# Re-placing the weight loads at the layer boundary of a two-layer decode kernel, and cutting its second query projection into three column groups

## The chip, the cores and the metric

The kernel runs on one core of one Trainium2 chip. The metric is the device time of one execution in microseconds (us). Most executions of one kernel agree within about 0.3%. Ratios below are computed as the mean time of one kernel's fast runs over that of the other's of the same rounds, so they are not quite the ratio of the medians that are quoted beside them.

In the profile lines PE is the matrix engine, PEld its weight loads, DVE the vector engine, ACT the scalar engine, POOL the GpSimd engine, and SP the engine on whose queue the loads are issued; L102 is line 102 of that kernel. 16 DMA engines move the bytes. "issue" is time in which an engine waited for nothing that the profile shows. A load has landed when all its bytes are there.

## The reference, cut to what matters

One token goes twice through an attention block and a gated feed-forward block, with the same weights and the same caches both times. Only the last 4096 of 32768 cache positions count.

```python
# D = 640, 32 heads of 192, window W = 4096, F = 1536, bf16
def _A_ref(x, k_cache, v_cache, wq, wo):
    q = (x @ wq).reshape(B, Sq, Hq, Dh) ...
    k = k_cache[:, :, Sk - W:, :]; v = v_cache[:, :, Sk - W:, :]
    scores = einsum("bhqd,bhkd->bhqk", q, k) * (Dh ** -0.5)
    o = einsum("bhqk,bhkd->bhqd", _softmax(scores), v)
    return o ... @ wo
def _B_ref(x, w1, w3, w2):
    return (_silu(x @ w1) * (x @ w3)) @ w2
x = x + _A_ref(_layernorm(x), ...); x = x + _B_ref(_layernorm(x), ...)
x = x + _A_ref(_layernorm(x), ...); x = x + _B_ref(_layernorm(x), ...)
```

K and V of the window are 100.7 MB together. They do not fit on the core, so most of them are loaded once for each layer.

## The kernel before

Heads go in four blocks of eight (b), each in four pairs (z). One large tile `pg` holds everything that is loaded: a work area for the probabilities, an area `AUX` for wo, a strip that keeps 20 of the 64 positions per partition of one V pair for the second layer, and seven slots of one K or V pair each (3 MB). Every load has a planned place. One function issues all of them, in one fixed order, on the SP queue. A load waits there until the readers of what was in its place are done, and all later loads wait behind it:

```python
    def need(key):
        while key not in place:
            k, at, n, src = queue.pop(0)
            ...
            nc.sync.dma_start(out=pg[:, at:at + n], in_=src)
```

The first layer handles its blocks in the order 0, 1, 2, 3 and the second in the order 3, 2, 1, 0. The K pairs of block 3 and most of its V are kept, so they fill all seven slots while the kernel passes from the first layer to the second. In that time the loads must live in the 12,288 columns below the kept strip: first wo of block 3, then w1, w3, w2 and the second layer's wq.

```python
    plan_cut(("wo", 0, 3), D, CUT_WO, wo_v[3], AUX)               # AUX = 4096
    plan_ffn(0, ((0, QCH, 2 * QCH), (7680, 0, 10752), QCH))       # w1, w3, w2; QCH = 3072
    for half, ring in ((1, (0, 1, 2, 3, 0)), (0, (1, 2, 3, 0, 1))):
        for c in range(NCH):                                      # wq in 10 chunks of 768 KB
            o = 6144 * c + 3072 * half
            plan(("wq", 1, half, c), QCH * ring[c], QCH, wq_v[:, o:o + 3072])
    ...
    plan_k(1, 2, 0, 1)      # the first K pair that the second layer loads: into slot 1
    ...
    wst = cst.tile([P, NZ, 2, 6, 36], BF16, name="wst")           # q, spread out as matmul weights
    ptm, e, et = pg[:, 0:2048], pg[:, 2048:3072], pg[:, 3072:4096]   # the work area
```

The second layer starts like this. The first half of wq (blocks 2 and 3) gives the weights `wst` for block 3, whose K is there already; `qproj_tail`, the "q tail", is the copy and the transposing matmuls that stand between. Each `k_stage` scores one kept K pair with 24 matmuls and so frees that pair's slot. The chunks of the other half are multiplied before and inside the first stage:

```python
            q_mms(q_ps[1], 1, (0,))
            st, rstd = statistics()
            q_mms(q_ps[1], 1, range(1, NCH))
            qproj_tail(q_ps[1], 1, rstd)
            q_mms(q_ps[0], 0, (0, 1))
            build_w(order[0])
            for z in range(NZ):
                between = [(6 + 4 * i, lambda c=c: q_mms(q_ps[0], 0, (c,))) for i, c in enumerate((2, 3))]
                k_stage(order[0], z, s_ps, z == 0, z == NZ - 1, between if z == 0 else ())
                if z == 0:
                    q_mms(q_ps[0], 0, (4,))
                    work_area()
```

## Time and profile before

| | |
|---|---|
| median time | 537.48 us (6 runs, 536.04 to 538.25) |
| span of the profiled run | 534.3 us; that run took 536.04 us, the shortest of all |
| loaded | 222 MB |
| rate in the steady parts | 420 to 440 GB/s |

Lines of the page of the kernel before: the span; the busy share of the DMA engines and their rate in 40 equal slices; the main queue; the chain of waits by engine.

```profile
span 534.3 us, 6605 instructions
...
DMA  8999999999999999999999989999999999999995
GB/s 353 442 423 426 440 422 432 436 421 434 430 423 425 438 429 437 424 426 430 418 355 397 400 339 422 424 434 425 432 430 423 434 429 432 432 428 429 417 409 222
...
q1 hardware_dynamic: 15554, 221.59, 98.1%
...
DMA 61%; DVE 15%; PE 13%; issue 7%; ACT 3%; SPq 1%; another core or an unknown queue 0%; ACTq 0%; DVEq 0%
```

The DMA engines are busy nearly always, and the rate is level but for slices 21 to 24 (355, 397, 400, 339), which is 267 to 321 us: the layer boundary. A closer look at it, in the kernel before. Each line is a stretch of 3 us; the last two numbers are the share of the DMA engines and GB/s, the number before them is the granted clock of PE.

```profile
273.00:276.00 3.00, 1.30 (x25) 1.07 (x22) 0.90 (x2) 0.48 (x1) 0.00 (x0) 0.50 0.86 301
276.00:279.00 3.00, 2.17 (x50) 2.04 (x51) 0.56 (x3) 0.00 (x0) 0.00 (x0) 0.50 0.87 278
291.00:294.00 3.00, 1.62 (x37) 1.46 (x35) 0.57 (x3) 0.00 (x0) 0.00 (x0) 0.50 1.00 353
294.00:297.00 3.00, 2.19 (x18) 1.05 (x19) 0.69 (x4) 0.41 (x2) 0.00 (x0) 0.50 0.97 381
312.00:315.00 3.00, 3.00 (x24) 1.01 (x20) 1.34 (x1) 0.00 (x0) 0.00 (x0) 1.00 0.58 160
315.00:318.00 3.00, 3.00 (x16) 0.83 (x14) 0.00 (x0) 0.00 (x0) 0.00 (x0) 1.00 0.84 360
```

These are three holes. When the loads were issued says why. This is the timeline of the SP queue of the kernel before (start, duration of the group from its first issue to its last, what, how many):

```profile
251.47 2.34 SPq L102 DMA_DIRECT2D pg<-in_A_v_cache_dram  x3
253.86 1.53 SPq L102 DMA_DIRECT2D pg<-in_A_wo_dram  x3
273.19 12.69 SPq L102 DMA_DIRECT2D pg<-in_B_w_dram  x9
287.35 18.09 SPq L102 DMA_DIRECT2D pg<-in_A_wq_dram  x10
306.98 0.33 SPq L102 DMA_DIRECT2D pg<-in_A_wo_dram  x1
312.95 0.56 SPq L102 DMA_DIRECT2D pg<-in_A_k_cache_dram  x1
```

And these are the longest waits of that queue between 270 and 330 us, in the kernel before (total us, times, longest):

```profile
SPq L102 <- PE s_ps L318: 20.1, 4, 5.6
SPq L102 <- PE o_ps L363: 17.7, 1, 17.7
```

Nothing is issued between 255 and 273 us, because w1's place is the work area, and the last matmul that reads the probabilities (`o_ps`) is still to come. In the second hole the second q load waits until 291.10 us, for the first two pieces of w2 to be multiplied. The K load at 312.95 waits for the first K stage (`s_ps`).

### The profile page before, as it was taken

To read this page: it belongs to the slowest core of one execution; us is meant where nothing else is said; L and a number is where in the kernel's file an instruction comes from. 1 tells how busy PE (TensorE), PEld (TensorE's weight loads), DVE (VectorE), ACT (ScalarE), POOL (GpSimd) and SP (SyncE) were. 2 spreads that over 40 slices of the span, in tenths; PEclk is the share of its full clock that TensorE was granted. 3 is DMA by queue.
4 is the path that set the end of the run, shared out by engine and by line. 5 is a ranking of instruction groups with operands and counts; after the bars stand their busy time and mean duration, and the time that the engine had idled before them with its cause. 6 is when DMAs were issued, how large, how long until landed. Compare 5 with 4: busy or idle time off the path is not lost.

```text
span 534.3 us, 6605 instructions
## 1 busy us (share of the span) xinstructions
PE 292.2 (55%) x2934; PEld 124.5 (23%) x2934; DVE 247.0 (46%) x287; ACT 37.9 (7%) x90; POOL 8.7 (2%) x38
## 2 busy tenths in 40 slices
PE   2427655550764416946366598584773425945475
PEld 1201111110321112213135232221321112312153
DVE  3169974426475074553011116788475175553011
ACT  0100020001100020002000001101100020002000
POOL 6000000000000000000000000000000000000000
PEclk9998877765678758867556599987777757977657
DMA  8999999999999999999999989999999999999995
GB/s 353 442 423 426 440 422 432 436 421 434 430 423 425 438 429 437 424 426 430 418 355 397 400 339 422 424 434 425 432 430 423 434 429 432 432 428 429 417 409 222
DMA packets 15726, 222.00 MB, mean 416 GB/s; under 512 B 1873, under 2 KB 1874, under 8 KB 7378
## 3 DMA queue, kind: packets, MB, share of 16 engines
q1 hardware_dynamic: 15554, 221.59, 98.1%
q8 instruction: 23, 0.38, 0.3%
q14 instruction: 5, 0.04, 0.0%
q10 hardware_dynamic: 144, 0.00, 0.0%
HBM read 221.58 MB, written 0.00 MB: 415 GB/s over the span
## 4 chain that ended last, share of the span: by engine, by line
DMA 61%; DVE 15%; PE 13%; issue 7%; ACT 3%; SPq 1%; another core or an unknown queue 0%; ACTq 0%; DVEq 0%
DMA pg<-in_A_k_cache_dram 43%; DVE pg L310 10%; PE s_ps L318 7%; DMA pg<-in_A_v_cache_dram 6%; DMA pg<-in_B_w_dram 5%; DMA pg<-in_A_wo_dram 5%; PE y_ps L395 3%; DMA pg<-in_A_wq_dram 2%; ACT pg L340 2%; DVE pg L343 1%; PE o_ps L363 1%; DVE wst L302 1%; ACT pg L351 1%; SPq L102 1%; PE z_ps L470 1%
## 5 line engine op out<-in xcount | busy, mean ns | idle before, releaser
L310 DVE STREAM_TRANSPOSE pg<-pg 128x1536 uint32<-128x1536 uint32 x112 | 189.1, 1746 | 108.5 <-DMA pg<-in_A_k_cache_dram 108.4
L318 PE MATMUL s_ps<-pg,wst 128*32 128x512 bf16 x768 | 174.6, 615 | 109.6 <-DVE pg L310 105.8
L318 PEld LDWEIGHTS <-wst 128*32 128x32 bf16 x768 | 47.2, 116 | 219.8 <-issue 202.9
L363 PE MATMUL o_ps<-pg 128*16 128x384 bf16 (+1 forms) x1024 | 75.1, 377 | 21.3 <-DMA pg<-in_A_v_cache_dram 18.2
L363 PEld LDWEIGHTS <-pg 128*16 128x16 bf16 (+1 forms) x1024 | 31.4, 97 | 51.9 <-issue 39.7
L340 ACT ACTIVATE pg<-s_ps,nbt 32x512 bf16<-32x512 f32 x16 | 13.2, 822 | 369.8 <-DVE nbt L337 369.6
L380 PE MATMUL ot_ps<-o_sb,csel 128*128 128x192 bf16 x16 | 3.5, 317 | 64.6 <-ACT o_sb L377 64.6
L395 PE MATMUL y_ps<-otd,pg 128*128 128x1 bf16 x540 | 23.3, 178 | 12.5 <-DVE otd L387 6.8
L282 PE MATMUL q_ps<-pg,xs 128*32 128x384 bf16 x160 | 16.5, 495 | 21.9 <-DMA pg<-in_A_wq_dram 21.9
L395 PEld LDWEIGHTS <-pg 128*128 128x128 bf16 x540 | 23.1, 131 | 14.5 <-issue 8.0
L384 DVE SCALAR_TENSOR_TENSOR om<-ot_ps,rl,dsel 128x192 f32<-128x192 f32 x8 | 3.1, 386 | 36.9 <-PE ot_ps L380 36.9
L372 DVE RECIPROCAL rl<-rl_ps 128x1 f32<-128x1 f32 x8 | 1.3, 168 | 38.0 <-PE rl_ps L370 38.0
L380 PEld LDWEIGHTS <-csel 128*128 128x128 bf16 x16 | 1.6, 99 | 68.1 <-issue 68.1
L343 DVE STREAM_TRANSPOSE pg<-pg 128x1024 bf16<-128x1024 bf16 x8 | 10.0, 1245 | 15.2 <-ACT pg L340 15.2
L351 ACT COPY pg<-pg 32x256 bf16<-32x256 bf16 x32 | 13.6, 424 | 8.0 <-DVE pg L343 7.5
L282 PEld LDWEIGHTS <-xs 128*32 128x32 bf16 x160 | 6.5, 123 | 28.4 <-issue 17.2
L298 DVE TENSOR_SCALAR qt_sb<-qt_ps,rstd 128x96 bf16<-128x96 f32 x4 | 1.3, 318 | 19.5 <-PE qt_ps L295 19.5
L328 DVE TENSOR_REDUCE t<-s_ps 128x1 f32<-128x512 f32 x8 | 5.2, 646 | 11.0 <-PE s_ps L318 11.0
L353 DVE COPY pg<-pg 32x256 bf16<-32x256 bf16 x32 | 9.2, 287 | 0.6
L434 PE MATMUL u_ps<-xn,pg 128*128 128x1 bf16 x120 | 7.7, 198 | 3.3 <-DMA pg<-in_B_w_dram 3.3
L434 PEld LDWEIGHTS <-pg 128*128 128x128 bf16 x120 | 7.4, 160 | 4.2 <-DMA pg<-in_B_w_dram 4.2
L222 POOL MEMSET pg<- 128x128 f32 x1 | 0.2, 204 | 481.9 <-PE o_ps L363 481.9
(73 smaller groups left out, 84.0 us busy)
## 6 DMA issues: line engine op xcount, KB each, us to landing
pg<-in_A_k_cache_dram SPq DMA_DIRECT2D x28, 3072.0 KB, 40.6
pg<-in_A_v_cache_dram SPq DMA_DIRECT2D x25, 3072.0 KB, 37.0
pg<-in_A_wo_dram SPq DMA_DIRECT2D x5, 1920.0 KB, 34.5
pg<-in_A_wq_dram SPq DMA_DIRECT2D x10, 768.0 KB, 6.8
pg<-in_A_wq_dram SPq DMA_DIRECT2D x2, 3072.0 KB, 13.3
pg<-in_A_wo_dram SPq DMA_DIRECT2D x9, 640.0 KB, 21.4
pg<-in_B_w_dram SPq DMA_DIRECT2D x7, 768.0 KB, 11.4
pg<-in_A_v_cache_dram SPq DMA_DIRECT2D x2, 2112.0 KB, 17.2
```

The costliest lines, as they stand in the source:

```text
L102: nc.sync.dma_start(out=pg[:, at:at + n], in_=src)
L282: nc.tensor.matmul(q_ps[32 * j:32 * j + 32, 0:384], lhsT=xs4[:, c, c2, :], rhs=w[:, o:o + 384], start=(c == 0 and cl == 0), stop=(c == NCH ...
L302: nc.vector.tensor_tensor(out=_ap(wst[:], 0, P, 4 + 216 * h, [[433, NZ], [36, 6], [8, 4]]), in0=_ap(qt_sb[:], 0, P, 96 * h + 4 * b, [[1, N ...
L310: nc.vector.transpose(v, v)
L318: nc.tensor.matmul(s_ps[64 * h:64 * h + 32, :], lhsT=wst[:, z, h, it, 4 - 4 * th:36 - 4 * th], rhs=_ap(x, 0, P, 192 * th + 64 * be + par + ...
L340: nc.scalar.activation(out=_ap(e, 64 * h, 32, h, [[32, 32], [2, 16]]), in_=s_ps[r, :].rearrange("p (t j) -> p t j", j=16), func=ACTF.Exp, ...
L343: nc.vector.transpose(et, e)
L351: nc.scalar.copy(out=dst, in_=src)
L353: nc.vector.tensor_copy(out=dst, in_=src)
L363: nc.tensor.matmul(o_ps[32 * j:32 * j + mw, 0:384], lhsT=ptm[:, po:po + mw], rhs=x[:, 384 * i:384 * i + 384], start=st, stop=(last and u > ...
L395: nc.tensor.matmul(y_ps[:, c:c + 1], lhsT=w[:, D * i + c:D * i + D:NCH], rhs=od[:, ci:ci + 1], start=(first and ci == 0 and c == 0), stop= ...
L434: nc.tensor.matmul(u_ps[:, f:f + 1], lhsT=w[:, FF * cl + f:FF * cl + FF:12], rhs=xn[:, c:c + 1], start=(c == 0 and f == 0), stop=(c == NCH ...
```

## The change

Its intent: let the first w1 pieces land where nothing is read any more, let q's pieces be finer and the first block's quarter come first, and multiply the rest between the matmuls of two K stages, so that K slots come free while q is still being loaded. The amount loaded is the same. For room, `wst` moves from a tile of its own to the head of `pg`, and the block-diagonal copies of x (`xs4`) become one narrow tile read at shifted columns (`xw`), which gives the same matmuls.

```diff
-AUX = WORK
+WST = NZ * 2 * 6 * 36
+AUX = WORK + WST
+KEPT = 14592
-KEPT = AUX + 8192
-QCH = 3072
+QC = 1536
-CUT_1 = (2, 2, 1)
+CUT_1 = ((1, 1, 1, 1, 1), (2, 2, 1))
+RING = dict(wo=((5312, 7872, 10432),),
+            w1=(0, 3776, 12992, 1728, 5312), w3=(6848, 9920, 12992), w2=(0, 2560, 5120),
+            q=((7872, 9408, 10944, 12992, 0), (1728, 4800, 7872, 10944, 1728), (4800, 6336, 7872, 9408, 10944)))
+QGROUPS = ((3, 1), (1, 2), (0, 1))
 ... (cut: the plan of the loads uses these places; wo of block 3, layer 1, is one load instead of three)
-    wst = cst.tile([P, NZ, 2, 6, 36], BF16, name="wst")
-    ptm, e, et = pg[:, 0:2048], pg[:, 2048:3072], pg[:, 3072:4096]
+    wst = pg[:, 0:WST].rearrange("p (z h i n) -> p z h i n", z=NZ, h=2, i=6)
+    ptm, e, et = pg[:, WST:WST + 2048], pg[:, WST + 2048:WST + 3072], pg[:, WST + 3072:WST + 4096]
 ... (cut: xw instead of xs4; qproj_mm and qproj_tail take a group; build_w takes a range of pairs;
      layer 0 gathers all of q in one PSUM tile, with one tail instead of two)
-            q_mms(q_ps[1], 1, range(1, NCH))
-            qproj_tail(q_ps[1], 1, rstd)
-            q_mms(q_ps[0], 0, (0, 1))
-            build_w(order[0])
-            for z in range(NZ):
-                ...
+            q_mms(qg[0], 0, range(1, NCH))
+            weight_area()
+            qproj_tail(qg[0], *QGROUPS[0], rstd)
+            build_w(order[0], 0, 1)
+            build_w(order[0], 1, 3)
 ...
+            chunks("b0")
+            k_stage(order[0], 0, s_ps, True, False, (at(3, "b1"), at(6, "b2"), at(9, "b3")))
+            chunks("b4")
+            k_stage(order[0], 1, s_ps, False, False, (at(3, "c0"), at(6, "c1", "c2")))
+            chunks("c3", "c4")
+            work_area()
+            k_stage(order[0], 2, s_ps, False, False)
+            qproj_tail(qg[1], *QGROUPS[1], rstd)
+            k_stage(order[0], 3, s_ps, False, True)
```

Here "b1" is chunk 1 of the second group, and `at(3, ...)` puts it after the third pair of matmuls of the stage.

More of the change, by code (lines that the diff above doesn't have):

```diff
@@ L31 @@
 SLOT = 64 * DH
+ZEROED = 3072
 WORK = 4096
-AUX = WORK
+WST = NZ * 2 * 6 * 36
+AUX = WORK + WST
+KEPT = 14592
 KEPT_T = 20
-KEPT = AUX + 8192
 SLOT0 = KEPT + KEPT_T * DH
@@ L147, in plan_ffn @@
     def plan_ffn(layer, at):
-        plan_cut(("w1", layer), FF, CUT_1, w1_v, at[0])
+        plan_cut(("w1", layer), FF, CUT_1[layer], w1_v, at[0])
         plan_cut(("w3", layer), FF, CUT_3[layer], w3_v, at[1])
@@ L168 @@
     plan_v(0, 3, 3, *cut_v(0))
-    plan_cut(("wo", 0, 3), D, CUT_WO, wo_v[3], AUX)
-    plan_ffn(0, ((0, QCH, 2 * QCH), (7680, 0, 10752), QCH))
-    for half, ring in ((1, (0, 1, 2, 3, 0)), (0, (1, 2, 3, 0, 1))):
+    plan_cut(("wo", 0, 3), D, CUT_WO, wo_v[3], RING["wo"][0])
+    plan_ffn(0, (RING["w1"], RING["w3"], RING["w2"]))
+    for g, (c2, n) in enumerate(QGROUPS):
         for c in range(NCH):
-            o = 6144 * c + 3072 * half
-            plan(("wq", 1, half, c), QCH * ring[c], QCH, wq_v[:, o:o + 3072])
-    def plan_wo3(i):
-        w = 4 * D
-        plan(("wo", 1, 3, i), AUX + i * w, w, wo_v[3][:, i * w:i * w + w])
-    plan_wo3(1)
+            o = 4 * QC * c + QC * c2
+            plan(("wq", 1, g, c), RING["q"][g][c], QC * n, wq_v[:, o:o + QC * n])
     plan_k(1, 2, 0, 1)
@@ L184 @@
     plan_k(1, 2, 2, 2)
-    plan_wo3(0)
-    plan_wo3(2)
+    plan_cut(("wo", 1, 3), D, (12,), wo_v[3], AUX)
     plan_k(1, 2, 3, 6)
@@ L213 @@
     nc.vector.memset(xsq[:, 11:12], EPS * D / P)
-    xs4 = cst.tile([P, NCH, 4, 32], BF16, name="xs4")
-    nc.vector.memset(xs4[:].rearrange("p c s n -> p (c s n)").bitcast(U32), 0)
-    nc.vector.memset(_ap(xs4[:], 0, P, 4, [[128, NCH], [33, 4]]), 1.0)
-    nc.vector.tensor_copy(out=_ap(xs4[:], 0, P, 0, [[128, NCH], [33, 4]]),
-                          in_=xb[:].unsqueeze(2).broadcast_to([P, NCH, 4]))
+    xw = cst.tile([P, NCH, 36], BF16, name="xw")
+    nc.vector.memset(xw[:].rearrange("p c n -> p (c n)").bitcast(U32), 0)
+    nc.vector.memset(xw[:, :, 7], 1.0)
+    nc.vector.tensor_copy(out=xw[:, :, 3], in_=xb[:])
     nc.vector.tensor_copy(out=xsq[:, 0:NCH], in_=xb[:])
@@ L275, in squares, with qproj_mm, qproj_tail @@
         nc.vector.tensor_tensor(out=xsq[:, 6:6 + NCH], in0=xsq[:, 0:NCH], in1=xsq[:, 0:NCH], op=ALU.mult)
-    def qproj_mm(q_ps, half, c, w, off):
-        for cl in range(2):
-            c2 = 2 * half + cl
+    def qproj_mm(q_ps, c, c2s, w, first, last):
+        for i, c2 in enumerate(c2s):
             for j in range(4):
-                o = off + 384 * (4 * cl + j)
-                nc.tensor.matmul(q_ps[32 * j:32 * j + 32, 0:384], lhsT=xs4[:, c, c2, :], rhs=w[:, o:o + 384],
-                                 start=(c == 0 and cl == 0), stop=(c == NCH - 1 and cl == 1),
+                o = 384 * (4 * i + j)
+                nc.tensor.matmul(q_ps[32 * j:32 * j + 32, 0:384], lhsT=xw[:, c, 3 - c2:35 - c2], rhs=w[:, o:o + 384],
+                                 start=(first and i == 0), stop=(last and i == len(c2s) - 1),
                                  tile_position=(0, 32 * j))
-    def qproj_tail(q_ps, half, rstd):
+    def qproj_tail(q_ps, c2, n, rstd):
         q_sb = wrk.tile([P, 384], BF16, tag="w0", name="q_sb")
         nc.scalar.copy(out=q_sb[:], in_=q_ps[:, 0:384])
-        qt_ps = ps_m.tile([P, 2, 6, 8], F32, tag="m", name="qt_ps")
+        qt_ps = ps_m.tile([P, 2, 6, 4 * n], F32, tag="m", name="qt_ps")
         for hh in range(2):
@@ L295, in qproj_tail, with build_w @@
                     nc.tensor.matmul(qt_ps[32 * a:32 * a + 32, hh, it, :], lhsT=q_sb[:, o:o + 63:2],
-                                     rhs=selm[:, 2 * half:2 * half + 2, :].rearrange("p c j -> p (c j)"),
+                                     rhs=selm[:, c2:c2 + n, :].rearrange("p c j -> p (c j)"),
                                      start=True, stop=True, tile_position=(0, 32 * a))
-        nc.vector.tensor_scalar_mul(out=qt_sb[:, :, :, 8 * half:8 * half + 8], in0=qt_ps[:], scalar1=rstd[:])
-    def build_w(b):
+        nc.vector.tensor_scalar_mul(out=qt_sb[:, :, :, 4 * c2:4 * c2 + 4 * n], in0=qt_ps[:], scalar1=rstd[:])
+    def build_w(b, z0=0, nz=NZ):
         for h in range(2):
-            nc.vector.tensor_tensor(out=_ap(wst[:], 0, P, 4 + 216 * h, [[433, NZ], [36, 6], [8, 4]]),
-                                    in0=_ap(qt_sb[:], 0, P, 96 * h + 4 * b, [[1, NZ], [16, 6], [0, 4]]),
-                                    in1=_ap(grp[:], 0, P, 0, [[0, NZ], [0, 6], [1, 4]]), op=ALU.mult)
+            nc.vector.tensor_tensor(out=_ap(wst, 0, P, 4 + 216 * h + 433 * z0, [[433, nz], [36, 6], [8, 4]]),
+                                    in0=_ap(qt_sb[:], 0, P, 96 * h + 4 * b + z0, [[1, nz], [16, 6], [0, 4]]),
+                                    in1=_ap(grp[:], 0, P, 0, [[0, nz], [0, 6], [1, 4]]), op=ALU.mult)
     def k_transpose(x):
@@ L401, in to_residual @@
     def to_residual(y_ps):
-        nc.vector.tensor_tensor(out=_ap(xs4[:], 0, P, 0, [[128, NCH], [33, 4]]),
-                                in0=xsq[:, 0:NCH].unsqueeze(2).broadcast_to([P, NCH, 4]),
-                                in1=_ap(y_ps[:], 0, P, 0, [[1, NCH], [0, 4]]), op=ALU.add)
+        nc.vector.tensor_tensor(out=xw[:, :, 3], in0=xsq[:, 0:NCH], in1=y_ps[:, 0:NCH], op=ALU.add)
         nc.vector.tensor_tensor(out=xsq[:, 0:NCH], in0=xsq[:, 0:NCH], in1=y_ps[:, 0:NCH], op=ALU.add)
@@ L410, in ffn_hidden @@
         c = 0
-        for i, n in enumerate(CUT_1):
+        for i, n in enumerate(CUT_1[layer]):
             w = need(("w1", layer, i))
@@ L414, in ffn_hidden @@
                 for j in range(4):
-                    nc.tensor.matmul(g_ps[32 * j:32 * j + 32, 0:384], lhsT=xs4[:, c, 0, :],
+                    nc.tensor.matmul(g_ps[32 * j:32 * j + 32, 0:384], lhsT=xw[:, c, 3:35],
                                      rhs=_ap(w, 0, P, FF * cl + 3 * j, [[12, 128], [1, 3]]),
@@ L478 @@
     squares()
-    nc.vector.memset(_ap(wst[:], 0, P, 0, [[1, NZ * 2 * 6 * 36]]).bitcast(U32), 0)
     for t in s_two:
@@ L483, in work_area, with weight_area @@
     def work_area():
-        live["work"] = (0, WORK)
-        nc.vector.memset(pg[:, 0:3072].bitcast(U32), 0)
+        live["work"] = (WST, WORK)
+        nc.vector.memset(pg[:, WST:WST + ZEROED].bitcast(U32), 0)
+    def weight_area():
+        live["wst"] = (0, WST)
+        nc.vector.memset(pg[:, 0:WST].bitcast(U32), 0)
+    weight_area()
     work_area()
@@ L510, in v_stage, with q_mms @@
                     done(k)
-        def q_mms(qh_ps, half, cs):
+        def q_mms(q_ps, g, cs):
+            c2, n = QGROUPS[g]
             for c in cs:
-                qproj_mm(qh_ps, half, c, need(("wq", 1, half, c)), 0)
-                done(("wq", 1, half, c))
-        q_ps = [ps_a.tile([P, 512], F32, tag="a", name=f"q_ps{i}") for i in range(2)]
+                qproj_mm(q_ps, c, range(c2, c2 + n), need(("wq", 1, g, c)), c == 0, c == NCH - 1)
+                done(("wq", 1, g, c))
         s_ps, l = s_two[0], ls[:, 0:1]
         if layer == 0:
+            q_ps = ps_a.tile([P, 512], F32, tag="a", name="q_ps")
             c = 0
@@ L523 @@
                 for cl in range(n):
-                    for half in range(2):
-                        qproj_mm(q_ps[half], half, c, w, 6144 * cl + 3072 * half)
+                    qproj_mm(q_ps, c, range(4), w[:, 4 * QC * cl:4 * QC * (cl + 1)], c == 0, c == NCH - 1)
                     c += 1
@@ L529 @@
                     st, rstd = statistics()
-            qproj_tail(q_ps[0], 0, rstd)
-            qproj_tail(q_ps[1], 1, rstd)
+            qproj_tail(q_ps, 0, 4, rstd)
             build_w(order[0])
@@ L536, with chunks, at @@
         else:
-            q_mms(q_ps[1], 1, (0,))
+            qg = [ps_a.tile([P, 512], F32, tag="a", name=f"qg_ps{g}") for g in range(3)]
+            q_mms(qg[0], 0, (0,))
             st, rstd = statistics()
-            q_mms(q_ps[1], 1, range(1, NCH))
-            qproj_tail(q_ps[1], 1, rstd)
-            q_mms(q_ps[0], 0, (0, 1))
-            build_w(order[0])
-            for z in range(NZ):
-                between = [(6 + 4 * i, lambda c=c: q_mms(q_ps[0], 0, (c,))) for i, c in enumerate((2, 3))]
-                k_stage(order[0], z, s_ps, z == 0, z == NZ - 1, between if z == 0 else ())
-                if z == 0:
-                    q_mms(q_ps[0], 0, (4,))
-                    work_area()
+            q_mms(qg[0], 0, range(1, NCH))
+            weight_area()
+            qproj_tail(qg[0], *QGROUPS[0], rstd)
+            build_w(order[0], 0, 1)
+            build_w(order[0], 1, 3)
+            def chunks(*names):
+                for name in names:
+                    q_mms(qg["abc".index(name[0])], "abc".index(name[0]), (int(name[1]),))
+            def at(n, *names):
+                return n, lambda: chunks(*names)
+            chunks("b0")
[7 more added lines that the diff above has]
+            k_stage(order[0], 3, s_ps, False, True)
         k_ready(order[1], 0)
@@ L556 @@
         if layer == 1:
-            qproj_tail(q_ps[0], 0, rstd)
+            qproj_tail(qg[2], *QGROUPS[2], rstd)
         y_ps = None
@@ L581 @@
             if layer == 0 and nxt is None:
-                del live["work"]
+                del live["work"], live["wst"]
             if nxt is not None:
@@ L600 @@
                     times_columns([("wo", layer, 1, 0)], (12,), later, y_ps, False, False)
-                cuts = CUT_WO if b in (last_b, 3) else (12,)
+                cuts = CUT_WO if b == last_b else (12,)
                 times_columns([("wo", layer, b, i) for i in range(len(cuts))], cuts, od, y_ps, bi == 0, bi == NB - 1)
```

## The prediction

> **What bounds the kernel now.** A stream of loads. The page's queue table gives 222 MB and 98.1% of the 16 DMA engines' span; the chain of waits is 61% DMA. Most of the 40 slices run at 420 to 440 GB/s. The Trainium skill ("DMA: Bandwidth & Descriptors", Specifications) puts the fabric ceiling at 435 GB/s; this trace agrees (one-microsecond bins reach 433). The change moves the same bytes, in the same order outside the layer boundary. It can win only where the load stream runs dry.
>
> **Where it runs dry.** Slices fall to 355, 397, 400 and 339 GB/s between 267 and 321 us. Stretches of 3 us show three holes:
> - 273 to 279 us: 301 and 278 GB/s. The first w1 load is issued only at 273.2: it lands in the work area and waits for layer 0's last PV matmul, while the queue holds just the wo pieces (the last lands at 277.0). Loss about 1.9 us.
> - 291 to 297: 353 and 381 (q chunks wait for w2 and w3 buffers). About 0.7 us.
> - 312 to 318: 160 and 360. Layer 1's first K load is issued at 312.95, when the first kept K has been scored; q chunks landing at 309.8 and 311.9 stand in that stage. About 2.9 us.
>
> With dents at 306 and 324 the sum is about 6.2 us, the ceiling of the gain.
>
> **What the change does.**
> - wst moves into the page, and w1 pieces find room that is free earlier. Three (1.18 MB, 2.8 us of stream) no longer touch the probabilities and queue behind wo before 270 us; the first hole closes.
> - q is cut by head columns: the first block's quarter first (5 x 384 KB), then the middle pair, then the last quarter, spread over two K stages. By my replay of the loads with durations from the trace (8 q matmuls 0.83 us, a K stage 5.2 to 5.8 us) the first K stage ends near 307 instead of 313, while q loads last until 309 to 310. The 2.9 us hole shrinks below 0.5; the 0.7 us one mostly goes.
> - A new hole: the next K load waits for the third kept K's scores (about 320.5) with the backlog ending near 322, and a 768 KB load into an empty queue took 4.5 us to land, 1.8 of it moving: 0.5 to 1.5 us.
> - Finer rows: packets of 3072 B ran at 398 GB/s over 16 engines (123 ns each), of 6144 B at 420 (median 234 ns). About 5.5 MB moves from 6 KB to 3 KB rows: +0.3 us.
> - wo as one load, one q tail fewer, a smaller residual write: under 0.2 us. The 6 us after the last load stay.
>
> All of it is on the critical path, since the queue is full before 273 and after 330. Net: 6.2 - 0.3 - about 1.2 left = 4.7 us.
>
> **Prediction.** 532.8 us, 8 in 10 between 530.5 and 535.5. Faster by over 2%: 0.02; within 2%: 0.97; slower: 0.01.
>
> **What shows it right.** w1 issued before 270 us; 273 to 279 above 390 GB/s; layer 1's first K load issued near 307; its first wo load landed near 342 (now 347.3); tail unchanged. **Wrong:** a hole over 1.5 us between 318 and 326, q stretches under 395 GB/s, or the saving vanishing between 345 and 520 (then compute sets the pace there).
>
> **What would make it wrong.** The score stage running slower at the granted clock of 0.5 it now starts in; interleaved q chunks stalling PE in order; small loads costing more than their packets.

## The result, and the profile after

The median is 530.52 us (529.94 to 532.33, 7 runs) against 537.59 us (536.04 to 539.33, 16 runs). The ratio is 0.9871, with a 95% interval of 0.9855 to 0.9887: 7.0 us less, where 4.7 were predicted. The number lies inside the predicted range by 0.02 us, far less than the runs scatter: that it lies inside is luck.

The same lines of the page of the changed kernel:

```profile
span 528.7 us, 6620 instructions
...
GB/s 357 426 434 433 427 432 430 429 431 428 433 427 427 435 431 429 431 426 432 419 406 403 421 421 434 423 434 428 433 425 431 431 433 428 434 425 435 413 412 209
...
q1 hardware_dynamic: 16274, 221.59, 98.7%
...
DMA 62%; DVE 16%; PE 16%; ACT 3%; issue 2%; SPq 1%; another core or an unknown queue 0%; ACTq 0%; DVEq 0%
```

The bytes are the same. Slices 21 to 24 are now 406, 403, 421, 421. "issue" fell from 7% to 2% of the chain. The same six stretches, in the changed kernel:

```profile
273.00:276.00 3.00, 1.47 (x27) 1.24 (x27) 0.90 (x2) 0.40 (x1) 0.00 (x0) 0.50 1.02 415
276.00:279.00 3.00, 2.73 (x49) 2.21 (x48) 0.59 (x4) 0.00 (x0) 0.00 (x0) 0.50 1.01 366
291.00:294.00 3.00, 2.37 (x29) 1.39 (x28) 1.19 (x7) 0.39 (x2) 0.00 (x0) 0.50 1.04 421
294.00:297.00 3.00, 1.56 (x54) 0.53 (x51) 0.63 (x1) 0.49 (x2) 0.00 (x0) 0.50 1.02 427
312.00:315.00 3.00, 3.00 (x17) 1.00 (x14) 0.00 (x0) 0.00 (x0) 0.00 (x0) 1.00 1.02 411
315.00:318.00 3.00, 3.00 (x64) 1.20 (x61) 0.73 (x2) 0.00 (x0) 0.00 (x0) 1.00 0.93 396
```

All three holes are gone but for a dent at 276 to 279. The SP queue of the changed kernel:

```profile
253.44 2.33 SPq L109 DMA_DIRECT2D pg<-in_A_wo_dram  x3
257.23 27.16 SPq L109 DMA_DIRECT2D pg<-in_B_w_dram  x11
284.85 19.00 SPq L109 DMA_DIRECT2D pg<-in_A_wq_dram  x15
305.04 0.55 SPq L109 DMA_DIRECT2D pg<-in_A_k_cache_dram  x1
311.28 0.53 SPq L109 DMA_DIRECT2D pg<-in_A_v_cache_dram  x1
316.83 6.11 SPq L109 DMA_DIRECT2D pg<-in_A_k_cache_dram  x2
```

The first w1 load is issued at 257 us instead of 273, and the first K load at 305 instead of 313.

To see where time is won, it helps to ask when the main queue had moved a given number of bytes. All these kernels load the same things in the same order up to 114 MB and after 144 MB. The table is summed from the DMA packets of each trace (us from the span's start; the last column is the difference of the outer two). The experiments' traces are in it too.

```
kernel          114 MB   120 MB   130 MB   132 MB   144 MB   114 to 144
before          268.62   285.14   310.29   318.50   346.88   78.26
before_2        268.62   285.07   311.33   319.69   348.08   79.46
before_3        268.59   285.37   311.89   320.54   348.84   80.25
changed         268.45   283.38   307.70   312.75   341.12   72.67
after_again     268.42   283.42   307.97   313.60   341.50   73.08
after_3         268.44   283.31   307.79   312.89   341.09   72.65
w1_late         268.36   287.02   311.09   316.08   344.70   76.34
w1_coarse       268.45   284.42   309.91   315.38   343.51   75.06
q_one_stage     268.42   283.26   307.50   316.96   345.38   76.96
two_groups      268.32   283.16   308.81   316.13   344.74   76.42
both_undone     268.36   286.25   310.36   319.91   348.13   79.77
before_spread   268.66   285.35   313.27   319.63   348.08   79.42
```

Up to 114 MB the kernels agree within 0.35 us. In the first pair of traces 5.6 us are won between 114 and 144 MB, and that is also the difference of their spans (534.3 and 528.7). What remained to be explained was why the medians differ by 7.0, and whether the holes were closed by what I had named. (By the order of the loads, V ends at 114 MB, wo at 116, w1 at 118, w3 at 120, w2 at 122 and q at 130.)

### The profile page after: what moved, and what is told of

Its sections match the earlier page's. It is cut to its first block, busy times and chain, and to the rows that moved or that the text cites. A ratio compares the mean times of both kernels' runs of the same rounds, so it can differ in the third digit from the quotient of the medians.

```text
span 528.7 us, 6620 instructions
## 1 busy us (share of the span) xinstructions
PE 293.9 (56%) x2934; PEld 126.0 (24%) x2934; DVE 247.2 (47%) x290; ACT 37.9 (7%) x90; POOL 8.7 (2%) x38
## 4 chain that ended last, share of the span: by engine, by line
DMA 62%; DVE 16%; PE 16%; ACT 3%; issue 2%; SPq 1%; another core or an unknown queue 0%; ACTq 0%; DVEq 0%
DMA pg<-in_A_k_cache_dram 41%; DVE pg L308 11%; DMA pg<-in_A_v_cache_dram 9%; PE s_ps L316 9%; DMA pg<-in_B_w_dram 6%; DMA pg<-in_A_wo_dram 5%; PE y_ps L393 3%; PE o_ps L361 2%; ACT pg L338 2%; DVE pg L341 1%; DMA pg<-in_A_wq_dram 1%; DVE pg L300 1%; SPq L109 1%; PE qg_ps L280 1%; PE z_ps L466 1%
## 5 line engine op out<-in xcount | busy, mean ns | idle before, releaser
L316 PE MATMUL s_ps<-pg 128*32 128x512 bf16 x768 | 176.9, 618 | 109.7 <-DVE pg L308 104.9
L316 PEld LDWEIGHTS <-pg 128*32 128x32 bf16 x768 | 48.1, 116 | 217.7 <-issue 199.5
L361 PE MATMUL o_ps<-pg 128*16 128x384 bf16 (+1 forms) x1024 | 76.3, 383 | 20.6 <-DMA pg<-in_A_v_cache_dram 17.5
L393 PE MATMUL y_ps<-otd,pg 128*128 128x1 bf16 x540 | 23.1, 178 | 11.5 <-DVE otd L385 6.8
L280 PE MATMUL q_ps<-pg,xw 128*32 128x384 bf16 x80 | 6.3, 483 | 15.7 <-DMA pg<-in_A_wq_dram 15.7
L280 PEld LDWEIGHTS <-xw 128*32 128x32 bf16 x160 | 6.8, 117 | 24.5 <-issue 14.6
L296 DVE TENSOR_SCALAR qt_sb<-qt_ps,rstd 128x48 bf16<-128x48 f32 (+2 forms) x4 | 1.3, 317 | 21.0 <-PE qt_ps L293 21.0
L280 PE MATMUL qg_ps<-pg,xw 128*32 128x384 bf16 x80 | 9.6, 410 | 1.7 <-DMA pg<-in_A_wq_dram 1.7
L326 DVE TENSOR_REDUCE t<-s_ps 128x1 f32<-128x512 f32 x8 | 5.2, 644 | 11.2 <-PE s_ps L316 11.2
## 6 DMA issues: line engine op xcount, KB each, us to landing
pg<-in_B_w_dram SPq DMA_DIRECT2D x10, 384.0 KB, 11.5
```

What stands on the lines that cost most here:

```text
L280: nc.tensor.matmul(q_ps[32 * j:32 * j + 32, 0:384], lhsT=xw[:, c, 3 - c2:35 - c2], rhs=w[:, o:o + 384], start=(first and i == 0), stop=(la ...
L316: nc.tensor.matmul(s_ps[64 * h:64 * h + 32, :], lhsT=wst[:, z, h, it, 4 - 4 * th:36 - 4 * th], rhs=_ap(x, 0, P, 192 * th + 64 * be + par + ...
L361: nc.tensor.matmul(o_ps[32 * j:32 * j + mw, 0:384], lhsT=ptm[:, po:po + mw], rhs=x[:, 384 * i:384 * i + 384], start=st, stop=(last and u > ...
L393: nc.tensor.matmul(y_ps[:, c:c + 1], lhsT=w[:, D * i + c:D * i + D:NCH], rhs=od[:, ci:ci + 1], start=(first and ci == 0 and c == 0), stop= ...
```

## The experiments

The theory (A) is that the load stream ran dry at three places because of waits for buffers, and that the new places of w1, the early quarter of q and the spread of the chunks closed them. The rivals: (B) less work on the compute engines, or the new addresses, made the gain; (C) the finer pieces of q did it by themselves; (D) the holes are not independent. For the size of the gain there were (E), that the kernel before usually loses more at the boundary than in its first trace, and (F), that the rest of the run varies.

### after_again: the changed kernel, unchanged

> The changed kernel again, unchanged, as the reference for the three kernels beside it. Every theory: 530 to 532 us, ratio to the kernel before 0.987. Theory A (the load stream no longer runs dry at three places of the layer boundary): 1-us bins between 273 and 319 us stay above 370 GB/s but for one dent near 277, and the stretch from 114 MB to 144 MB of loads takes 72.7 us, as in the first trace of it, against 78.3 in the trace of before.

It took 530.85 us (median of 4 runs), ratio 0.9858 (0.9835 to 0.988). The stretch from 114 to 144 MB took 73.08 us. One sign failed: beside the dent at 277 to 280 us (347, 349 and 368 GB/s in bins of 1 us) there is a second one at 308 to 311 us (354, 354 and 348), which the first trace of the changed kernel does not have; I have no cause for it. This run is the reference for w1_late, q_one_stage and both_undone, which ran on the same chip.

### w1_late: w1 waits again

```diff
-            w1=(0, 3776, 12992, 1728, 5312), ...
+            w1=(1728, 5312, 12992, 0, 3776), ...
```

> The changed kernel, but the first w1 piece lands where the probabilities lie and the second where the first wo piece of block 3 lies, so w1 waits as it did before. Theory A: w1 is issued at about 273 us, the hole of 273 to 279 us comes back, 1.9 us longer than the changed kernel (1.0 if only the wait for the last PV matmul counts). Rival B (the gain comes from less work on the compute engines, such as one q tail fewer and the smaller residual write, or from the new addresses): no difference over 0.5 us.

It took 534.75 us, ratio 0.9932 (0.9912 to 0.9952): 3.9 us longer than the changed kernel beside it. Two lines of its SP queue, and its rate in the hole:

```profile
253.33 2.23 SPq L109 DMA_DIRECT2D pg<-in_A_wo_dram  x3
270.82 16.41 SPq L109 DMA_DIRECT2D pg<-in_B_w_dram  x11
```

```profile
273.00:282.00 9.00, 5.49 (x80) 3.76 (x80) 2.39 (x10) 0.60 (x3) 0.00 (x0) 0.50 0.78 261
```

The changed kernel moves 396 GB/s in the same 9 us and the kernel before 324. So the places of w1 alone are worth microseconds, and rival B fails here: the compute work and the set of addresses are the same, and only which w1 piece takes which place was permuted. But the edit overdid it. The first piece went out at 270.8 us, since its columns hold only the first probabilities, and then the second waited for the first wo piece to be multiplied (275.56). Each piece is small (384 KB), and they went out one at a time into a dry queue, so the hole is larger than that of the kernel before. The 3.9 us are thus not the size of the first hole's gain.

### w1_coarse: w1 in three pieces again

```diff
-CUT_1 = ((1, 1, 1, 1, 1), (2, 2, 1))
+CUT_1 = ((2, 2, 1), (2, 2, 1))
-            w1=(0, 3776, 12992, 1728, 5312), ...
+            w1=(0, 3072, 12992), ...
```

> The changed kernel, but layer 0's w1 in three pieces (768, 768 and 384 KB) as before, the first on the place of wst and the first probabilities, the second over the rest of the work area and 832 columns of the first wo piece. Theory A: the second piece waits for that wo piece (275.8 us), a hole of 1.0 to 2.0 us stands near 275 to 279, so the kernel takes 1.0 to 2.0 us longer than the changed one (ratio 0.989 to 0.991 where the changed one has 0.987). If only the wait for the last PV matmul mattered: under 0.5 us longer.

It took 533.24 us, ratio 0.9913 (0.9895 to 0.9931), about 2.7 us longer than the changed kernel (median against median, on different chips; 2.3 by the ratios). The mechanism was as expected and the size larger. At 120 MB it is 1.0 us behind the first trace of the changed kernel, at 130 MB 2.2 us, at 144 MB 2.4 us: less than half of the loss falls in the hole itself. Loads issued late are consumed late, and the next loads wait for their places; that this is the whole of the rest is argued, not tested. I had counted the holes as independent, and in this run they are not.

### q_one_stage: all chunks inside the first K stage

```diff
-            chunks("b0")
-            k_stage(order[0], 0, s_ps, True, False, (at(3, "b1"), at(6, "b2"), at(9, "b3")))
-            chunks("b4")
-            k_stage(order[0], 1, s_ps, False, False, (at(3, "c0"), at(6, "c1", "c2")))
-            chunks("c3", "c4")
+            chunks("b0", "b1")
+            k_stage(order[0], 0, s_ps, True, False, (at(3, "b2"), at(5, "b3"), at(7, "b4"), at(8, "c0"),
+                                                     at(9, "c1"), at(10, "c2"), at(11, "c3", "c4")))
+            k_stage(order[0], 1, s_ps, False, False)
```

> The changed kernel, but all q chunks are multiplied before the end of the first kept K stage, as before; sizes and order of the loads unchanged. Theory A: the stage ends when the last q chunk has landed and been multiplied, near 310.5 us, so the first K load of layer 1 is issued then and not at 305; a hole of 2 to 3 us opens near 309 to 313, and the kernel is 2.0 to 2.9 us longer than the changed one. Rival C (the smaller q pieces and their order alone closed the hole): under 0.7 us longer.

It took 535.17 us, ratio 0.9943 (0.9929 to 0.9958), 4.3 us longer than the changed kernel beside it. Its SP queue and its rate:

```profile
284.76 18.83 SPq L109 DMA_DIRECT2D pg<-in_A_wq_dram  x15
310.04 0.56 SPq L109 DMA_DIRECT2D pg<-in_A_k_cache_dram  x1
```

```profile
306.00:318.00 12.00, 10.92 (x62) 3.36 (x60) 0.81 (x1) 0.00 (x0) 0.00 (x0) 1.00 0.71 283
```

The q loads are the same fifteen, in the same order, and issued at the same times. Only the K load is 5.0 us later, and the 12 us run at 283 GB/s instead of 427. Rival C fails for this hole: finer pieces without the spread do not close it. (For the second hole it is in part right, see below.) The loss was larger than I had said, because the stream stood still longer than the last landing (309.2) tells: in bins of 1 us the rate was 230, 84, 0, 0 and 83 GB/s from 307 us on. Some DMA engines ran empty well before the last one had finished, and the first packets of the K load appear only at 311.4 us.

### both_undone

It has both edits, of w1_late and of q_one_stage.

> Both edits together. Theory A with holes that add up: 4 to 5 us longer than the changed kernel, so 1.5 to 3 us of the total gain of 7 stay unexplained by these two holes (the 291 to 297 hole was 0.7 us). Theory D (holes absorb each other, since what is issued late in the first shifts the second): less than the sum of the two single edits by over 1 us. Rival B: no difference.

It took 538.03 us, ratio 1.0001 (0.9985 to 1.0017): all of the gain is gone, though the single q tail of layer 0, the smaller residual write, wst's new place, the single wo load and the three groups are still in it. So less compute does not carry the gain (B). The loss is far over the 4 to 5 us expected. The single edits cost 3.9 and 4.3 us, together 8.2; both cost 7.2. The difference would be the overlap (D), but 1 us is no more than the intervals of these ratios (about 0.002, or 1 us, each way), so D is not shown. That the loss of both equals the gain is partly luck, since both edits make larger holes than the kernel before has: 251 GB/s against 324 between 273 and 282 us, and 276 against 323 between 306 and 318. A small gain of the parts that are left can hide behind that, and the table has one: from 120 to 130 MB, the stretch of the second hole, this kernel takes 24.1 us like the changed one (24.3 to 24.6), and the kernel before 25.1 to 26.5. w1_late and q_one_stage take 24.1 and 24.2, too, but two_groups, with q in pieces of 768 KB, 25.7. So the gain in the second hole does not hang on w1's order or on the spread; it goes with the finer q pieces, the early quarter, or both, and late w1 loads can spoil it (25.5 in w1_coarse).

### before_spread: only the spread, in the kernel before

```diff
-            q_mms(q_ps[0], 0, (0, 1))
             build_w(order[0])
-            for z in range(NZ): ...
+            k_stage(order[0], 0, s_ps, True, False, (q_at(4, 0), q_at(8, 1)))
+            q_mms(q_ps[0], 0, (2,))
+            k_stage(order[0], 1, s_ps, False, False, (q_at(4, 3), q_at(8, 4)))
+            work_area()
+            k_stage(order[0], 2, s_ps, False, False)
+            k_stage(order[0], 3, s_ps, False, True)
```

> The kernel before, with its loads, addresses and q halves as they were, but the five chunks of the second q half spread over two kept K stages. If spreading the chunks is what frees the first K buffer, the first K load of layer 1 is issued near 310.5 us instead of 313 and 2.0 us are won, ratio 0.996; the rest of the third hole's gain needs the finer q groups. If spreading alone does it all: 3.2 us, 0.994. If the finer groups do it all: under 0.5 us.

It took 538.16 us, ratio 1.0006 (0.9981 to 1.0031): nothing was won in the whole, and my guess of 2.0 us was wrong. The SP queue shows the first K load at 313.85, and below it stand the last q load alone and the rate around it, each first in the kernel before and then here:

```profile
287.88 22.39 SPq L102 DMA_DIRECT2D pg<-in_A_wq_dram  x10
312.05 0.33 SPq L102 DMA_DIRECT2D pg<-in_A_wo_dram  x1
313.85 0.55 SPq L102 DMA_DIRECT2D pg<-in_A_k_cache_dram  x1
```

```profile
305.11 0.33 SPq L102 DMA_DIRECT2D pg<-in_A_wq_dram  x1
309.95 0.33 SPq L102 DMA_DIRECT2D pg<-in_A_wq_dram  x1
309.00:312.00 3.00, 3.00 (x28) 1.19 (x27) 0.00 (x0) 0.00 (x0) 0.00 (x0) 0.92 0.97 395
309.00:312.00 3.00, 3.00 (x25) 1.51 (x23) 0.00 (x0) 0.00 (x0) 0.00 (x0) 0.74 0.57 172
```

The first K stage began at 306.9 us, where it began at 306.7, 307.8 and 308.6 in three traces of the kernel before. It cannot begin earlier: it needs the whole first half of wq (3.9 MB, landed at 303.8 here), then the copy, the transposing matmuls and wst. Nor does it get shorter, since two chunks are still multiplied inside it.

But the edit also made a hole of its own. The last q load takes the place of the second half's first chunk, which is multiplied here only inside the stage; so it was issued at 309.95 us, where the three traces of the kernel before issued it at 305.11, 306.27 and 306.89. By the table, the stretch from 130 to 132 MB took 6.4 us instead of 8.4 in the mean, the 2.0 us that I had guessed, and the stretch from 120 to 130 MB took 27.9 instead of 26.0. So this run does not show that the spread is worth nothing without the early quarter; it shows that with the old places it gives back in the q loads what it wins at the K load. A spread with other places for the chunks was not tried.

### two_groups: only the spread, in the changed kernel

```diff
-QGROUPS = ((3, 1), (1, 2), (0, 1))
+QGROUPS = ((2, 2), (0, 2))
-            q=((7872, 9408, 10944, 12992, 0), (1728, 4800, 7872, 10944, 1728), (4800, 6336, 7872, 9408, 10944)))
+            q=((7872, 10944, 0, 3072, 7872), (10944, 1728, 4800, 7872, 10944)))
 ... the second group's five chunks are spread over the first two stages
```

> The changed kernel with q in two groups (the blocks 2 and 3 first, then 0 and 1) in chunks of 768 KB instead of three groups, the second group still spread over two kept K stages. If the early quarter is needed, because the first kept K stage can begin only when its whole group has landed, been copied and turned into wst: that stage begins near 304.5 us instead of 298.5, the first K load is issued near 310 instead of 305, and the kernel is 2.5 to 4 us longer than the changed one (ratio 0.992 to 0.995). If spreading is what counts in the changed kernel: under 0.7 us longer.

It took 533.93 us, ratio 0.9931 (0.9912 to 0.995), some 3.2 us longer than the changed kernel by the ratios (0.9931 against 0.9871, on different chips). Its SP queue and rate:

```profile
285.73 19.89 SPq L109 DMA_DIRECT2D pg<-in_A_wq_dram  x10
309.20 0.55 SPq L109 DMA_DIRECT2D pg<-in_A_k_cache_dram  x1
```

```profile
306.00:318.00 12.00, 12.00 (x83) 6.54 (x77) 1.34 (x1) 0.00 (x0) 0.00 (x0) 1.00 0.87 340
```

Two halves make the first K stage begin at 302.6 us, and three groups at 298.0. The first K load follows 6.6 to 7.0 us later in both (309.2 and 305.0). So both count in the changed kernel: without the spread it loses 4.3 us, and without the quarter some 3.2. The second run changes the size of the q pieces as well, and does not tell the two apart: it is 1.2 us slower than the changed kernel (mean of three traces) from 120 to 130 MB and 2.1 us slower from 130 to 132 MB, where the later first stage shows. Two lines of PE show the early start, first in the kernel before, then in the changed one (start, time, what, how many matmuls):

```profile
306.70 1.92 PE L318 MATMUL s_ps<-pg,wst 128*32 128x512 bf16 x7
```

```profile
298.02 1.57 PE L316 MATMUL s_ps<-pg 128*32 128x512 bf16 x6
```

### before_2, before_3 and after_3: what a single trace hid

No edit; one run each, state unknown, all within 0.5% of the medians.

> The kernel before again, one look, for a second trace: its first trace was of the run of 536.04 us, the shortest of 16 (median 537.6). Theory E (the load stream's holes at the layer boundary vary from run to run and were small in that run): the stretch from 114 MB to 144 MB of loads is over 79 us here (78.3 in the first trace), and explains the longer span. Theory F (the rest of the run varies): that stretch within 0.4 us of 78.3, the rest longer.

> The kernel before once more, for a third trace. Theory E: the stretch from 114 to 144 MB over 79 us; theory F: within 0.4 us of 78.3 and the rest longer.

> The changed kernel again, one look, for a third trace of it. Theory E (the kernel before loses more in most runs than in its first trace, through loads that wait for one another; the changed one is steadier): the stretch from 114 MB to 144 MB takes 72.5 to 73.3 us here, against 78.3, 79.5 and 80.3 in three traces of before.

They took 537.21, 537.69 and 531.60 us. The stretch from 114 to 144 MB took 79.46 and 80.25 us in the kernel before, and 72.65 in the changed one. From 144 MB to the end the three traces of the kernel before differ by 0.2 us (187.4, 187.3, 187.2). So E holds: the kernel before varies at the boundary, and its first trace, of its shortest run, was the best of the three there. The three traces of the changed kernel agree within 0.5 us at the boundary. They differ more in the rest (187.6, 189.2 and 188.8 us from 144 MB to the end). In the mean that is 1.2 us longer than in the kernel before, and all of it comes after 220 MB, in the last loads and the tail behind them (10.2, 11.5 and 11.2 us against 9.8, 9.7 and 9.6). I have no cause for it.

The variation sits in the q loads. This is the stretch from 282 to 306 us in the first and the third trace of the kernel before, and then in the changed kernel:

```profile
282.00:306.00 24.00, 13.00 (x225) 8.85 (x222) 3.56 (x15) 1.57 (x5) 0.00 (x0) 0.57 1.01 403
```

```profile
282.00:306.00 24.00, 12.08 (x217) 8.53 (x214) 2.25 (x12) 1.57 (x5) 0.00 (x0) 0.50 0.98 374
```

```profile
282.00:306.00 24.00, 18.87 (x264) 12.34 (x266) 4.51 (x19) 1.96 (x6) 0.00 (x0) 0.60 1.02 413
```

In the kernel before, a q load takes 5 to 8 us from issue to landing, and there are four places of 768 KB. A new load is issued only when a chunk has landed and been multiplied, about 1 us later, so a late landing delays the load four places on. The trace shows this coupling; that it is why the runs differ is an inference.

With the means of three traces each, the gain at the boundary can be told by place:

```
stretch           before   changed   gain, us   what is in it
114 to 120 MB     16.58    14.93     1.65       wo, w1, most of w3
120 to 130 MB     25.98    24.45     1.53       end of w3, w2, nearly all of q
130 to 132 MB      8.41     5.26     3.15       last of q, first K load
132 to 144 MB     28.36    28.16     0.20       K, V, wo
sum               79.33    72.80     6.53
```

## Why the prediction was right or wrong

The forecast of "within 2%" and the range held: 530.52 us in 530.5 to 535.5, but by 0.02 us, which is luck. The gain was 7.0 us and not 4.7. The mechanism was right; the terms of the sum that were mis-sized are "about 1.2 left" and the ceiling of 6.2 us.

- **What bounds the kernel, and where it runs dry:** right. All but 0.2 us of the gain that the traces show lies between 114 and 144 MB of loads, at the three named holes.
- **First hole** ("about 1.9 us"; "three w1 pieces queue behind wo before 270 us"): right. They were issued at 257.2, 264.5 and 268.2 us, and the gain there is 1.65 us. The sign that 273 to 279 would run above 390 GB/s held only in the mean (391); the second half had 366: the fifth and sixth loads behind wo (the last w1 piece and the first of w3) still wait, until 275.8 and 276.8, for wo pieces to be multiplied. I had placed the end of the backlog by the last landing. In the changed kernel's packets, those of 3072 B, which only w1 has there, begin at 272.8 us, and those of 5120 B, which only wo has there, still begin until 275.9. So the DMA engines seem to be some 3 us apart, and the foremost to run dry that much earlier. The Trainium skill ("DMA: Bandwidth & Descriptors", Queues, rings and completion order) says that on each engine descriptors are consumed in ring order, which agrees with this reading; the packets carry no engine number here, so it is inferred.
- **Second hole** ("about 0.7 us"): under-sized. The gain from 120 to 130 MB is 1.53 us in the mean; in the first pair of traces it is 0.8. I read the loss from one trace, whose run was the shortest of 16. The two later traces of the kernel before take 1.1 and 1.4 us more from 120 to 130 MB than the first.
- **Third hole** ("about 2.9 us"; the first stage "ends near 307"): right in size (3.15 us) and in mechanism, the wait for the first stage. The stage ran from 298.0 to 305.0, and the K load went out at 305.04. One detail does not stand: the q chunks that landed at 309.8 and 311.9 did not hold up the stage of the kernel before. Its chain has no such wait; the chunk that counted landed at 306.07, before the stage.
- **"A new hole ... 0.5 to 1.5 us":** this step failed most plainly. My replay put the q chunks and the K stages in series on PE and had the third stage end at 320.5; it ended at 316.8. In the stages two score matmuls start every 0.43 us, and a chunk of eight matmuls between them delays the next ones by 0.4 to 0.6 us (four chunks in the trace), not by the 0.83 us that it takes alone. The next K load went out with V still coming in until 321.8, and the bins of 1 us between 318 and 326 fall below 410 GB/s once (391).
- **Finer rows "+0.3 us":** about right. Packets of 3072 B took 121 ns in the median and those of 6144 B 234, so 1792 more of the small ones (768 before, 2560 after) over 16 engines cost (121 - 117) x 1792 / 16 ns = 0.45 us.
- **"About 1.2 left"**, and with it the sum: wrong. Of the ceiling of 6.2 us read from the first trace, 5.6 were won in the first pair, so 0.6 were left, the cost of the finer rows included, and not 1.5. With the mean of the traces as the baseline, the sum is 1.65 + 1.53 + 3.15 + 0.20 = 6.5 us. The three traced runs of the changed kernel give 1.2 us of it back after 144 MB, so the traced runs differ by 5.5 us in the mean (536.98 and 531.49), and the medians of all runs by 7.0. Two of the three traced runs of the changed kernel are slower than its median; the rest of the difference stays open.
- **"6.2 us, the ceiling of the gain":** a ceiling read from one trace holds for that trace only. There 5.6 us were won; in the median 7.0.
- **Landing of layer 1's first wo load near 342, and tail unchanged:** right in the first traces (341.4 us; from 221.5 MB to the end 5.6 us before and 5.7 after). In the two other traces of the changed kernel the tail took 6.4 and 6.5 us, against 5.6 and 5.2 in those of the kernel before.
- **The risk that the scores run slower at the granted clock of 0.5:** it did not come. Two score matmuls started every 0.43 us at 298 us, where the clock was 0.50, and at 314 us, where it was 1.00.

Shown on the chip, by undoing each: the places of w1 and the spread matter, and so does the early quarter together with its finer pieces; less compute does not carry the gain. Only argued: how much the quarter does without the finer pieces, and why the q stretch varies from run to run.

## What to carry to other kernels

In a kernel bound by a stream of loads, look for the loads that wait for a buffer, and ask what must finish before the buffer is free; moving a piece to a place that is free earlier, or splitting a projection so that its first consumer can start on a quarter, can win back the time for which the stream stood still. Undo parts from the full version as well as adding them to the old one, and when a part wins nothing alone, look in its trace for a wait that it has made: here the spread won 2 us at the K load and lost as much because a q load then waited for its place. Before a hole of a few microseconds is sized, take several traces: a run of the kernel with waits that feed on one another may lose 2 us more than the one that was traced.

## What the Trainium skill lacked or had wrong

- "DMA: Bandwidth & Descriptors", Specifications and Where 436 GB/s comes from: it gives about 358 GB/s as the HBM limit of a core and says that this side binds for loads from HBM. There the condition is missing; the page's section Bandwidth has it, where its single-core table (425 GB/s at 16 MB) is said to hold with the other core of the pair idle. With this one core running, 428 GB/s were held from 112 to 273 us, and bins of 1 us reach 433 and never more, close under its fabric ceiling of 435 GB/s.
- The same page, Latency and other measured facts: it gives about 600 ns to the first byte for loads issued from SP. The page does not say from where it counts. From the start of the issuing instruction, which itself takes about 0.55 us, to the first packet of a K load into an empty queue it was 1.33 to 1.37 us in five traces, so about 0.8 us from the instruction's end.
- The same page, Anatomy of one DMA: its fit of 2.0 us plus bytes over 436 GB/s is for the other issuing path, and an estimate from it is 3.8 us for 768 KB; the page has none for loads issued from SP. The quickest of such loads took 4.2 to 4.6 us to land (in a hole or after it, in four traces).
- The same page, Why small descriptors are slow: it gives a fixed overhead for each packet, with a descriptor of 256 B as its example, and no durations of large ones. Medians of 121 ns for 3072 B, 234 for 6144 B and 913 for 24,576 B lie on a line with 8 ns per row, so rows of 3 KB still run about 6% slower than rows of 24 KB.
- No page says how far the 16 engines drift apart in a long stream. The packets at 273 to 276 us speak for some 3 us here (inferred, without engine numbers); by this reading a load must be issued that much earlier to keep the foremost engine busy.
